# An attention and MLP kernel whose instruction order is laid out by a list scheduler of its own

## The chip, the core and the metric

The kernel runs on one core of a Trainium2 chip. A core has five engines with a queue each: TensorE (PE, matrix multiplication; its weight loads are shown as PEld), VectorE (DVE), ScalarE (ACT), GpSimd (POOL), and SyncE (SP), which here only issues DMA transfers. Each engine works through its own queue in the order in which the program was written out, and waits at an instruction until that instruction's inputs are there. The metric is the device time of one execution in microseconds.

## The reference

Four batches, eight heads, 768 positions, head size 64. Queries and keys are assigned to one of 16 centroids per head; a query attends only to keys with its own centroid. The attention output, as 3072 tokens of 512 numbers, goes through an MLP with 2048 hidden units.

```python
q_assign = np.argmax(np.einsum('bhsd,hcd->bhsc', q_n, c_n), axis=-1)
k_assign = np.argmax(np.einsum('bhsd,hcd->bhsc', k_n, c_n), axis=-1)
mask = q_assign[:, :, :, None] == k_assign[:, :, None, :]
scores = np.where(mask, scale * np.matmul(q, k.transpose(0, 1, 3, 2)), -1000000000.0)
attn = softmax(scores)                       # written out in the reference
x = matmul(attn, v) as (B * S, H * D)
g = s * np.maximum(x @ w_in, 0.0) ** 2 + b
out = g @ w_out
```

Inputs are float32. Most products are computed as three float16 products of a high and a low part.

## The kernel before

The work is cut into 192 attention units, each one head and 128 query positions of one batch (`units`), and 192 MLP steps, eight for each of 24 token tiles of 128 (`steps`; step m computes two of the 16 hidden tiles).

A unit `i` goes through these lines. `scores` (L492): four matmuls of 384 columns into one of two PSUM tiles `sc`; the one-hot encoding of the centroids rides along as extra rows (`KB`, `QB`), so that it masks. `maxima` (L501): the row maximum, VectorE. `exps` (L508, L511): a bias on VectorE, then the exponential on ScalarE into `p`. `high` (L519): the high half `ph` on ScalarE. `low` (L533, L535): the low half on GpSimd, and a transposing DMA from `ph` into `PT`. `values` (L552 to L564): for two units together, 36 matmuls into `px`, and the division on VectorE. Every fourth unit `finish_x` (L584 to L592) makes the MLP's input `x` through another transposing DMA, and every eighth, one matmul `am_x` (in `allmax`, L107) spreads a maximum over the partitions. The first 16 units ("raw") skip the halves: they are turned on TensorE in float32 (L530, L547), and the first two token tiles of the MLP are computed in float32 as well (L629, L673).

An MLP step runs `mlp_in` (L633, 24 matmuls of 128 columns into `h`), every second step `mlp_relu` (L646 to L649, ScalarE) and `mlp_g` (L661, GpSimd), and `mlp_out` (L676, six matmuls of 512 columns into `acc`); the end of a token tile is scaled on VectorE (L688) and stored (L690). Step m runs beside unit m + 14, its output three steps later (`LAG`, `BEHIND`).

Beside these run generators, advanced a little at each unit: `prep_q`, `prep_k` and `prep_v` prepare the next q, k and v (loads, maxima, halves, transposing DMAs into `QA`, `QB`, `KA`, `KB`; small matmuls `pq` L426 and `pk` L381 into a PSUM tile; `onehot` L309 to L315), `weights` decodes the 32 weight tiles (`fetch`, `rebase` L211 to L213 on ScalarE, `narrow` L217 and L218 on VectorE, `bound` L231 to L239), `wsplit` (L286 to L290) splits them into float16 halves.

Buffers come from rings named by a tag. Twelve "big" buffers hold `p`, `ph`, `PT`, `r` and the raw q. In PSUM there are two `sc`, one `acc`, one `h`, and two "m" tiles, which `px`, `pq`, `pk`, `am` and the weights' `pw` share.

The order of the queues comes from the framework's scheduler, which simulates the program with its own durations and takes what is ready by priority, the position in the program. The kernel steers it by hand in four ways: `first_of_all` moves the units 0 to 19 300 places forward; `behind(...)` holds instructions of the start behind others on the same engine (the one-hot, the turned tiles, the scale, the split); `gated` does so for the weights; and `load` holds each load behind the last transposing DMA.

Of the kernel before, what the change touches and what calls it, by code (L numbers as in the profile page):

```python
# [24 lines left out]

@with_exitstack
def tile_cluster_attention_mlp(ctx, tc, q, k, v, cent, w_in, w_out, s_in, b_in, out):
# [14 lines left out]
    V = nc.vector  # L42
    G = nc.gpsimd
    A = nc.scalar
# [33 lines left out]
    last_transpose = [None]  # L78
    last_split = [None, None]
    last_scale = [None]  # L80
    last_hot = [None]
    hot = [None]
    turned = [None]
    last_turn = [None]
    last_score = [None]
    last_max = [None]
    last_exp = [None]
# [15 lines left out]
    def allmax(dst, src, name):  # L103
        n = src.shape[1]
        pm = ps_m.tile([P, 512], F32, tag="m", name=f"am_{name}")
        for j in range(n):
            nc.tensor.matmul(pm[:, j * P : (j + 1) * P], src[:, j : j + 1].broadcast_to([P, P]), identb, start=True, stop=True)  # L107
        V.tensor_reduce(dst, pm[:, : n * P].rearrange("p (n q) -> p n q", q=P), axis=AX.X, op=ALU.max)
# [24 lines left out]
    def scalar_in(src, name):  # L133
        every = const([P, 1], F32, name)
        nc.sync.dma_start(every, src.partition_broadcast(P))
        return every

    def behind(*last):
        stack = ExitStack()
        for ins in last:  # L140
            if ins is not None:
                stack.enter_context(tc.issue_after(ins.ins))
        return stack

# [3 lines left out]
    nc.sync.dma_start(cn, cent.rearrange("h c d -> (h c) d"))  # L148
# [23 lines left out]
    for e in range(3):  # L172
        nc.tensor.matmul(pc[:, e * P : (e + 1) * P], cnat[:, e].rearrange("p e d -> p (e d)"), ident16, start=True, stop=True)
# [16 lines left out]
    def split(hi, lo, src, f):  # L190
        last_split[1] = A.activation(hi, src, AF.Copy, scale=f)
        yield
        V.scalar_tensor_tensor(lo, src, f, hi, op0=ALU.mult, op1=ALU.subtract)
# [29 lines left out]
    def bound(d):  # L223
        w, p, ft = d["w"], d["p"], d["ft"]
        top = w.bitcast(BF16).rearrange("p a (f z) -> p a f z", z=2)[:, :, :, 1]
        if p % 2:
# [4 lines left out]
            nc.tensor.matmul(sums[g], ones, top, start=ft in (0, EARLY), stop=done)  # L231
            if done:
                V.tensor_reduce(glob[:, 8 + g : 9 + g], sums[g], axis=AX.X, op=ALU.max)
        else:
            pw = ps_m.tile([P, 512], F32, tag="m", name=f"pw_{ft}")
            for t in range(KT):
                nc.tensor.matmul(pw[:, :P], ones, top[:, t, :], start=(t == 0), stop=(t == KT - 1))  # L237
# [7 lines left out]
    def gated(i):  # L245
        return behind(hot[0], turned[0]) if i < 20 else nullcontext()

    def weights():
        live = {}
        for i in range(2 * NF + 3):  # L250
            if 0 <= i - 3:
                with behind(last_score[0] if i < 20 else None):
                    bound(live[i - 3])
                narrowed[0] += 1
            if 0 <= i - 2 < 2 * NF:
                with gated(i):
                    narrow(live[i - 2])
            if i < 2 * NF:
                live[i] = fetch(i)
            if 0 <= i - 1 < 2 * NF:  # L260
                with gated(i):
                    rebase(live[i - 1])
# [32 lines left out]
    def column_sums():  # L295
        pb = ps_m.tile([P, 512], F32, tag="m", name="pb")
        for ft in range(NF):
            for e in range(2):
                nc.tensor.matmul(pb, ones16, WSP[ft][1][:, e, :], start=(ft + e == 0), stop=(ft + e == NF))
# [4 lines left out]
    def onehot(pa, nb, name, dst, mul, add):  # L304
# [10 lines left out]
        last_hot[0] = V.tensor_scalar(dst, o.unsqueeze(2).broadcast_to([P, nb, 4, C]), mul, add, op0=ALU.mult, op1=ALU.add)  # L315
# [3 lines left out]
    def turn(dst, src, early):  # L319
        if not early:  # L320
            return nc.sync.dma_start_transpose(dst, src)
        n = dst.shape[1]
        for a in range(0, n, 8):
# [4 lines left out]
            for j in range(a, z):  # L328
                nc.tensor.transpose(pt[:, (j - a) * P : (j - a + 1) * P], src[:, j * P : (j + 1) * P], ident16)
            last_turn[0] = A.activation(dst[:, a:z].rearrange("p n q -> p (n q)"), pt[:, : (z - a) * P], AF.Copy)  # L330
# [12 lines left out]
    def prep_k(b, hp):  # L343
# [18 lines left out]
        last_scale[0] = inverse2(V, sm[3], sm[2], 22)  # L362
# [3 lines left out]
        last_split[0] = G.tensor_copy(kb[:, :, :, 0, :], ka[:, :, :, 0, :])  # L366
# [9 lines left out]
        for h in range(2):  # L376
            hc = slice((2 * hp + h) * C, (2 * hp + h + 1) * C)
            for t in range(T):
                i = h * T + t
                o = pa[:, i * C : (i + 1) * C]  # L380
                nc.tensor.matmul(o, KA[:, i, :], cT[:, 0, hc], start=True, stop=False)  # L381
                nc.tensor.matmul(o, KA[:, i, :], cT[:, 1, hc], start=False, stop=True)
# [4 lines left out]
    def prep_q(b, c, hq):  # L387
# [21 lines left out]
        last_split[1] = A.activation(qb[:, :, 0, :], rows, AF.Copy)  # L409
        yield  # L410
        eng = G if b + c else V
        last_split[0] = eng.tensor_tensor(qa[:, :, 0, :], rows, qb[:, :, 0, :], op=ALU.subtract)
# [8 lines left out]
        for h in range(nh):  # L421
            hc = slice((nh * hq + h) * C, (nh * hq + h + 1) * C)
            for t in range(QT):
                i = h * QT + t
                o = pa[:, i * C : (i + 1) * C]
                nc.tensor.matmul(o, QA[:, i, :], cT[:, 0, hc], start=True, stop=False)  # L426
                nc.tensor.matmul(o, QA[:, i, :], cT[:, 2, hc], start=False, stop=True)
# [9 lines left out]
    def prep_v(b):  # L437
# [10 lines left out]
        for hp in range(NP):  # L448
            with behind(last_max[0] if b == 0 else None):
                absmax(vm[:, hp : hp + 1], vns[hp].rearrange("p h t d -> p (h t d)"))  # L450
# [32 lines left out]
    def scores(i):  # L483
# [5 lines left out]
        for X, Y, st in ((QA, KA, True), (QB, KB, False)):  # L489
            y = Y.rearrange("p n q -> p (n q)")  # L490
            for e in range(2):
                last_score[0] = nc.tensor.matmul(  # L492
# [4 lines left out]
    def maxima(i):  # L497
# [3 lines left out]
        last_max[0] = V.tensor_reduce(SM[i // 4][:, 0, j : j + 1], U[i]["sc"], axis=AX.XY, op=ALU.max, negate=True)  # L501

    def exps(i):
# [7 lines left out]
        last_exp[0] = A.activation(p.rearrange("p (a b) -> p a b", a=2), u["sc"], AF.Exp, bias=bi, scale=u["scale"], **total)  # L511
# [9 lines left out]
    def low(i):  # L521
        u = U[i]
        if i < RAW:
# [3 lines left out]
            for e, (pool, bank) in enumerate(((ps_h, "h"), (ps_m, "m"))):  # L527
                back = pool.tile([P, 512], F32, tag=bank, name=f"turned_{i}_{e}")
                for kt in range(n):
                    nc.tensor.transpose(back[:, kt * P : (kt + 1) * P], u["p"][:, (e * n + kt) * P : (e * n + kt + 1) * P], ident)  # L530
# [4 lines left out]
        last_transpose[0] = nc.sync.dma_start_transpose(u["PT"], u["ph"].rearrange("p e s -> p (e s)"))  # L535

    def values(i):
# [3 lines left out]
        for e in range(2):  # L541
# [3 lines left out]
            if i < RAW:  # L545
                for kt in range(T):
                    nc.tensor.matmul(o, PT[:, kt, :], VN[hp][:, h, kt, :], start=(kt == 0), stop=(kt == T - 1))  # L547
# [3 lines left out]
            for kt in range(T):  # L551
                nc.tensor.matmul(o1, PT[:, kt, :], vh[:, h, kt, : D + 1], start=(kt == 0), stop=False)  # L552
                nc.tensor.matmul(o, PT[:, kt, :], vl[:, h, kt, :], start=False, stop=False)  # L553
                nc.tensor.matmul(o1, PT[:, T + kt, :], vh[:, h, kt, : D + 1], start=False, stop=(kt == T - 1))  # L554
# [12 lines left out]
    def finish_x(g):  # L567
# [3 lines left out]
        if 4 * g < XRAW:  # L571
            xt = ps_m.tile([P, 512], F32, tag="m", name=f"xt_{g}")
            for j in range(2):
                nc.tensor.transpose(xt[:, j * P : (j + 1) * P], xs[:, j].rearrange("p h d -> p (h d)"), ident)
# [14 lines left out]
        nc.sync.dma_start_transpose(x.rearrange("p j e q -> p (j e) q"), xn.rearrange("p j e h d -> p (j e h d)"))  # L589
# [28 lines left out]
    def mlp_in(n, m):  # L618
# [3 lines left out]
        for j in range(2):  # L622
            ft = 2 * m + j
            o = ph[:, (2 * (m % 2) + j) * P :][:, :P]
            if plain(n):
                while narrowed[0] < 2 * ft + 2:
                    next(wgen, None)
                for kt in range(KT):
                    nc.tensor.matmul(o, wi[ft][:, kt, :], XS[(n, kt // 2)][:, kt % 2, :], start=(kt == 0), stop=(kt == KT - 1))  # L629
                continue  # L630
            terms = [(kt, wl, xl) for kt in range(KT) for wl, xl in ((0, 0), (0, 1), (1, 0))]
            for i, (kt, wl, xl) in enumerate(terms):
                nc.tensor.matmul(o, WSP[ft][0][:, wl, kt, :], XS[(n, kt // 2)][:, kt % 2, xl, :],  # L633
# [30 lines left out]
    def mlp_out(n, m):  # L664
# [4 lines left out]
        for j in range(2):  # L669
            ft = 2 * m + j  # L670
            rows = slice((2 * (m % 2) + j) * P, (2 * (m % 2) + j + 1) * P)
            if plain(n):
                nc.tensor.matmul(acc, g[:, rows], wo[ft].rearrange("p a f -> p (a f)"), start=(ft == 0), stop=(ft == NF - 1))  # L673
                continue
            for gl, wl in ((0, 0), (0, 1), (1, 0)):
                nc.tensor.matmul(acc, g[:, gl, rows], WSP[ft][1][:, wl, :],  # L676
# [3 lines left out]
        if m == STEPS - 1:  # L680
# [9 lines left out]
            nc.sync.dma_start(out[b * S : (b + 1) * S].rearrange("(p t) e -> p t e", t=T)[:, t, :], o)  # L690
# [31 lines left out]
    def first_of_all(k):  # L722
        return tc.high_priority(offset=300) if k < URGENT else nullcontext()

# [9 lines left out]
    def prepare(k):  # L734
        with behind(hot[0]):
            if k == 1:
                run(first_q[1])
                run(first_k[2])
            if k == 3:
# [120 lines left out]
```

## Time and profile before

| | |
|---|---|
| median of 3 runs | 994.08 us (992.73 to 995.89) |
| profiled execution | 997.6 us |
| its span, first to last instruction | 995.7 us |
| TensorE busy | 868.6 us, 87% of the span |
| VectorE busy | 643.5 us, 65% |
| ScalarE busy | 630.0 us, 63% |
| GpSimd busy | 519.2 us, 52% |
| mean granted TensorE clock | 0.963 |
| DMA queue of the data, share of 16 engines | 72.5% |

The span is what the trace covers. "Busy" leaves out waiting and the issuing of transfers. In the rows below, an instruction is named by the engine, the tile it writes and the line; `out<-in` names the tiles; x is a count; the number after the bar is the total busy time in us, then the mean of one in ns, then the idle time of the engine just before such instructions and what ended it. The granted clock is the share of full speed at which TensorE was let run.

### The profile page before, as it was taken

To read this page: it belongs to the slowest core of one execution; us is meant where nothing else is said; L and a number is where in the kernel's file an instruction comes from. 1 tells how busy PE (TensorE), PEld (TensorE's weight loads), DVE (VectorE), ACT (ScalarE), POOL (GpSimd) and SP (SyncE) were. 2 spreads that over 40 slices of the span, in tenths; PEclk is the share of its full clock that TensorE was granted. 3 is DMA by queue.
4 is the path that set the end of the run, shared out by engine and by line. 5 is a ranking of instruction groups with operands and counts; after the bars stand their busy time and mean duration, and the time that the engine had idled before them with its cause. 6 is when DMAs were issued, how large, how long until landed. Compare 5 with 4: busy or idle time off the path is not lost.

```text
span 995.7 us, 26540 instructions
## 1 busy us (share of the span) xinstructions
PE 868.6 (87%) x10883; PEld 646.2 (65%) x10885; DVE 643.5 (65%) x1704; ACT 630.0 (63%) x921; POOL 519.2 (52%) x443
## 2 busy tenths in 40 slices
PE   2547799988898989989888989989869989999997
PEld 2336677756566767766666767766656767767775
DVE  7868974797868564657776655576676565564420
ACT  4768865658656667656557666666557667667632
POOL 2225433335555656655465666665556566566631
PEclk9968799999999999999999999999999999999999
DMA  5824436648789878788989679789979778777730
GB/s 175 306 70 159 123 59 103 153 80 165 142 160 159 151 124 149 141 168 160 182 139 176 128 130 144 154 170 164 176 146 168 122 131 138 144 129 121 125 56 22
DMA packets 400682, 139.66 MB, mean 140 GB/s; under 512 B 386224, under 2 KB 386224, under 8 KB 400560
## 3 DMA queue, kind: packets, MB, share of 16 engines
q1 hardware_dynamic: 400560, 137.97, 72.5%
q8 instruction: 85, 1.39, 0.6%
q14 instruction: 37, 0.30, 0.1%
HBM read 35.69 MB, written 6.29 MB: 42 GB/s over the span
## 4 chain that ended last, share of the span: by engine, by line
PE 38%; DVE 18%; issue 14%; DMA 12%; POOL 11%; ACT 6%; SPq 1%; POOLq 0%; ACTq 0%; DVEq 0%
PE h L633 12%; PE acc L676 11%; POOL ph L533 5%; PE sc L492 5%; DVE ssm L501 3%; DMA qn<-in_q_dram 3%; DMA PT<-ph 2%; POOL g L661 2%; PE px L552 2%; ACT ph L519 2%; PE px L554 2%; DMA QA<-qa 2%; PE px L553 2%; DMA QB<-qb 1%; ACT p L511 1%
## 5 line engine op out<-in xcount | busy, mean ns | idle before, releaser
L533 POOL TENSOR_TENSOR ph<-p,ph 128x768 f16<-128x768 f32 x176 | 292.2, 1661 | 275.1 <-ACT ph L519 263.7
L511 ACT ACTIVATE p<-sc,ssm,qsm 128x768 f32<-128x768 f32 x192 | 189.3, 986 | 167.7 <-DVE ssm L508 94.4
L633 PEld LDWEIGHTS <-ws 128*128 128x128 f16 x4224 | 258.3, 99 | 42.3 <-issue 4.7
L676 PE MATMUL acc<-ws,g 128*128 128x512 f16 x1056 | 267.9, 382 | 13.3 <-POOL g L661 12.4
L633 PE MATMUL h<-x,ws 128*128 128x128 f16 x4224 | 277.5, 221 | 1.1 <-DVE ws L289 0.7
L501 DVE TENSOR_REDUCE ssm<-sc 128x1 f32<-128x768 f32 x192 | 182.5, 951 | 89.3 <-PE sc L492 89.1
L519 ACT ACTIVATE ph<-p 128x768 f16<-128x768 f32 x176 | 147.1, 836 | 27.4 <-DMA PT<-ph 15.6
L676 PEld LDWEIGHTS <-g 128*128 128x128 f16 x1056 | 96.9, 98 | 101.0 <-POOL g L661 15.9
L661 POOL TENSOR_TENSOR g<-r,g 128x512 f16<-128x512 f32 x88 | 104.1, 1183 | 29.7 <-ACT r L649 16.5
L552 PE MATMUL px<-vh,PT 128*128 128x65 f16 x1056 | 113.3, 197 | 3.1 <-DMA PT<-ph 1.1
L492 PE MATMUL sc<-KA,QA 128*128 128x384 f16 x384 | 97.1, 335 | 19.1 <-ACT p L511 18.1
L553 PE MATMUL px<-vl,PT 128*128 128x64 f16 x1056 | 113.1, 194 | 0.0
L554 PE MATMUL px<-vh,PT 128*128 128x65 f16 x1056 | 112.6, 195 | 0.0
L552 PEld LDWEIGHTS <-PT 128*128 128x128 f16 x1056 | 99.5, 99 | 8.3 <-issue 3.1
L492 PE MATMUL sc<-KB,QB 128*128 128x384 f16 x384 | 102.4, 335 | 1.7 <-DMA QB<-qb 1.1
L553 PEld LDWEIGHTS <-PT 128*128 128x128 f16 x1056 | 99.4, 100 | 4.2 <-issue 1.0
L554 PEld LDWEIGHTS <-PT 128*128 128x128 f16 x1056 | 99.4, 98 | 0.9
L646 ACT ACTIVATE r<-h,cf 128x512 f32<-128x512 f32 x88 | 60.1, 683 | 47.2 <-PE h L633 45.6
L239 POOL TENSOR_TENSOR w<-w,wsg 128x512 f32<-128x512 f32 x32 | 41.1, 1289 | 72.6 <-PE pw L237 33.2
L560 DVE TENSOR_SCALAR ssm<-px 128x2 f32<-128x2 f32 x88 | 13.5, 154 | 88.3 <-PE px L554 88.3
L492 PEld LDWEIGHTS <-QA 128*128 128x128 f16 x384 | 32.1, 100 | 42.0 <-issue 26.0
L587 POOL TENSOR_TENSOR xn<-xs,xn 128x256 f16<-128x256 f32 x44 | 31.5, 717 | 47.2 <-ACT xn L584 47.0
(167 smaller groups left out, 1271.5 us busy)
## 6 DMA issues: line engine op xcount, KB each, us to landing
wst<-in_moe_w_in_dram SPq DMA_DIRECT2D x16, 512.0 KB, 4.7
wst<-in_moe_w_out_dram SPq DMA_DIRECT2D x16, 512.0 KB, 5.0
kn<-in_k_dram SPq DMA_DIRECT2D x16, 384.0 KB, 4.1
qn<-in_q_dram SPq DMA_DIRECT2D x24, 256.0 KB, 4.3
vn<-in_v_dram SPq DMA_DIRECT2D x16, 384.0 KB, 4.0
out_dram<-o SPq DMA_DIRECT2D x24, 256.0 KB, 2.3
PT<-ph SPq DMA_TRANSPOSE x176, 3.9
x<-xn SPq DMA_TRANSPOSE x44, 2.9
```

The source lines that it names most:

```text
L492: last_score[0] = nc.tensor.matmul(sc[:, e, :HALF], X[:, col, :], y[:, h * S + e * HALF : h * S + (e + 1) * HALF], start=st, stop=not st)
L501: last_max[0] = V.tensor_reduce(SM[i // 4][:, 0, j : j + 1], U[i]["sc"], axis=AX.XY, op=ALU.max, negate=True)
L511: last_exp[0] = A.activation(p.rearrange("p (a b) -> p a b", a=2), u["sc"], AF.Exp, bias=bi, scale=u["scale"], **total)
L519: A.activation(u["ph"][:, 0, :], u["p"], AF.Copy)
L533: G.tensor_tensor(u["ph"][:, 1, :], u["p"], u["ph"][:, 0, :], op=ALU.subtract)
L552: nc.tensor.matmul(o1, PT[:, kt, :], vh[:, h, kt, : D + 1], start=(kt == 0), stop=False)
L553: nc.tensor.matmul(o, PT[:, kt, :], vl[:, h, kt, :], start=False, stop=False)
L554: nc.tensor.matmul(o1, PT[:, T + kt, :], vh[:, h, kt, : D + 1], start=False, stop=(kt == T - 1))
L633: nc.tensor.matmul(o, WSP[ft][0][:, wl, kt, :], XS[(n, kt // 2)][:, kt % 2, xl, :], start=(i == 0), stop=(i == len(terms) - 1))
L646: A.activation(r, ph, AF.Relu, scale=MS[n][0])
L661: G.tensor_tensor(g[:, 1, :], r, g[:, 0, :], op=ALU.subtract)
L676: nc.tensor.matmul(acc, g[:, gl, rows], WSP[ft][1][:, wl, :], start=(ft == 0 and gl + wl == 0), stop=(ft == NF - 1 and gl == 1))
```

## The change

The kernel body no longer issues instructions. Its engines are replaced by recorders (`V`, `G`, `A`, `M`, `S_`), and every call becomes a `Step` with the tiles that it reads and writes; from overlapping bytes the plan derives which earlier steps it must wait for. Matmuls in a row that write the same tile with the same weight tile become one step. At the end `plan.emit()` walks the steps in time with durations of its own: `takes` for the compute engines, `transfer` for DMAs. On each engine, among the steps whose inputs are done, it takes the one that can start first; those that could start within 30 ns of the engine coming free count as equal, and the earlier in the program goes first. A step can start only when its tiles have a buffer, and the buffers of a tag are given in the order in which the program first mentions them. It also models that VectorE and GpSimd exclude each other for some operations, and that no more than eight transfers are under way. The instructions are then issued in the order of their planned start, and the framework is told to keep it.

All hand-made steering is removed: `behind`, `gated`, `first_of_all`, the holding back of loads, and the variables that remembered instructions for it.

```diff
+class Plan:
+    LIGHT = 2.4
+    SIGNAL = 40.0
...
+    def record(self, queue, method, args, kwargs):
...
+        key = (id(writes[0].tensor), id(reads[0].tensor)) if queue.name == "PE" else None
+        step = self.last_pe
+        if key is None or step is None or step.key != key:
+            step = Step()
...
+    def takes(self, step):
+        method, args, kwargs = step.calls[0]
+        aps = [a for a in args if isinstance(a, bass.AP)]
+        if step.queue.name == "PE":
+            total = 0.0
+            for _, args, _ in step.calls:
+                n = self.width(args[0])
+                if args[1].dtype == F32:
+                    total += max(n * 4 / self.LIGHT, 112.0)
+                else:
+                    total += 56.0 if n == P else max(n / self.LIGHT + 2.5, 26.0)
+            return total, False
...
+        if name == "DVE":
+            if method in ("tensor_reduce", "reciprocal"):
+                return 145 + n / 0.96, method == "reciprocal" and not banks
+            if method == "tensor_tensor":
+                return 148 + n / 0.96, not banks
+            if method == "scalar_tensor_tensor":
+                return (200.0 if n == 1 else 165 + n * 1.1), not banks
+            fold = 1 if banks else 4 if small else 2
+            return 150 + n / 0.96 / fold, not banks
+        if name == "ACT":
+            more = 110 if "accum_out" in kwargs else 0
+            if banks:
+                return (170 + n * 0.84 if small else 140 + n * 1.1 if n > 700 else 130 + n * 0.97) + more, False
+            return (100 + n * 1.1 if args[2] == AF.Copy and "scale" in kwargs else 100 + n * 1.0) + more, False
+        if method == "tensor_tensor":
+            return 165 + n * 1.93, True
+        if method == "tensor_copy":
+            return 60 + n * 1.35, True
+        return 100.0, True
+
+    def transfer(self, step):
...
+        if method == "dma_start":
+            n = P * self.width(ap) * (2 if ap.dtype in (F16, BF16) else 4)
+            return 420.0, 1300.0, n / 410.0, 1050.0
+        n = self.width(ap) // P
+        return (1300.0 if n < 12 else 1480.0), 1300.0, n * 165.0, 500.0
+
+    def order(self):
...
+        while left:
+            best = None
+            for q, line in pending.items():
+                now = clock[q]
+                choice = None
+                for k in line:
+                    at, need = max(ready[k], now), {}
+                    for t in steps[k].tiles:
+                        if t.name in held:
+                            continue
+                        tag = self.tag(t)
+                        if turn[t.name] != given[tag] + need.get(tag, 0) or len(spare[tag]) <= need.get(tag, 0):
+                            at = None
+                            break
+                        at = max(at, spare[tag][need.get(tag, 0)])
+                        need[tag] = need.get(tag, 0) + 1
+                    if at is None:
+                        continue
+                    if q == "SP" and len(landed) >= 8:
+                        at = max(at, landed[-8])
+                    mine = (max(at, now + 30), self.weight[k], at, k)
+                    if choice is None or mine < choice:
+                        choice = mine
+                if choice and (best is None or choice[2] < best[2]):
+                    best = choice + (q,)
...
+            for j in after[k]:
+                open_[j] -= 1
+                same = steps[j].queue.name == q == "PE"
+                ready[j] = max(ready[j], end - 60 if same else end + self.SIGNAL)
...
+        return sorted(range(len(steps)), key=lambda k: (started[k], k))
...
+    def emit(self):
+        self.weight = [s.rank for s in self.steps]
+        for k in self.order():
+            s = self.steps[k]
+            for method, args, kwargs in s.calls:
+                self.tc.keep_in_program_order(getattr(s.queue.engine, method)(*args, **kwargs))
...
-    V = nc.vector
-    G = nc.gpsimd
-    A = nc.scalar
+    plan = Plan(tc)
+    V = plan.queue("DVE", nc.vector)
+    G = plan.queue("POOL", nc.gpsimd)
+    A = plan.queue("ACT", nc.scalar)
+    M = plan.queue("PE", nc.tensor)
+    S_ = plan.queue("SP", nc.sync)
...
-    def load(dst, src, free=False):
-        if last_transpose[0] is None or free:
-            nc.sync.dma_start(dst, src)
-        else:
-            with tc.issue_after(last_transpose[0].ins):
-                nc.sync.dma_start(dst, src)
+    def load(dst, src):
+        S_.dma_start(dst, src)
...
-    def gated(i):
-        return behind(hot[0], turned[0]) if i < 20 else nullcontext()
...
-                with behind(last_score[0] if i < 20 else None):
-                    bound(live[i - 3])
+                bound(live[i - 3])
...
-                with gated(i):
-                    narrow(live[i - 2])
+                narrow(live[i - 2])
...
-    def first_of_all(k):
-        return tc.high_priority(offset=300) if k < URGENT else nullcontext()
...
         if i < NU:
-            with first_of_all(i):
-                scores(i)
+            scores(i)
...
+    plan.emit()
```

More of the change, by code (lines that the diff above doesn't have):

```diff
@@ L1 @@
 import math
[L2 removed]
+import heapq
 import concourse.bass as bass
@@ L134, in scalar_in @@
         every = const([P, 1], F32, name)
-        nc.sync.dma_start(every, src.partition_broadcast(P))
+        S_.dma_start(every, src.partition_broadcast(P))
         return every
[L138 to L143, printed above, removed]
     ct = sb.tile([P, 2, D], F32, tag="r", name="ct", bufs=2)
     cn = ct[:, 0, :]
-    nc.sync.dma_start(cn, cent.rearrange("h c d -> (h c) d"))
+    S_.dma_start(cn, cent.rearrange("h c d -> (h c) d"))
     csq = ct[:, 1, :]
@@ L230, in bound @@
             done = ft in (EARLY - 1, NF - 1)
-            nc.tensor.matmul(sums[g], ones, top, start=ft in (0, EARLY), stop=done)
+            M.matmul(sums[g], ones, top, start=ft in (0, EARLY), stop=done)
             if done:
@@ L236, in bound @@
             for t in range(KT):
-                nc.tensor.matmul(pw[:, :P], ones, top[:, t, :], start=(t == 0), stop=(t == KT - 1))
+                M.matmul(pw[:, :P], ones, top[:, t, :], start=(t == 0), stop=(t == KT - 1))
             V.tensor_reduce(w1[:, ft : ft + 1], pw[:, :P], axis=AX.X, op=ALU.max)
@@ L448, in prep_v @@
         for hp in range(NP):
-            with behind(last_max[0] if b == 0 else None):
-                absmax(vm[:, hp : hp + 1], vns[hp].rearrange("p h t d -> p (h t d)"))
+            absmax(vm[:, hp : hp + 1], vns[hp].rearrange("p h t d -> p (h t d)"))
             if hp < NP - 1:
@@ L546, in values @@
                 for kt in range(T):
-                    nc.tensor.matmul(o, PT[:, kt, :], VN[hp][:, h, kt, :], start=(kt == 0), stop=(kt == T - 1))
+                    M.matmul(o, PT[:, kt, :], VN[hp][:, h, kt, :], start=(kt == 0), stop=(kt == T - 1))
                 continue
@@ L734, in prepare @@
     def prepare(k):
[L735 to L739, printed above, removed]
-                run(first_k[3])
-            if k == 2:
-                some(first_v, 2)
-            if k == 6:
-                active.append(first_v)
+        if k == 1:
+            run(first_q[1])
+            run(first_k[2])
+        if k == 3:
+            run(first_k[3])
+        if k == 2:
+            some(first_v, 2)
+        if k == 6:
+            active.append(first_v)
     first_v = prep_v(0)
@@ L754, in tile_cluster_attention_mlp @@
     some(first_k[0], 2)
-    with behind(last_scale[0]):
-        some(first_k[1], 1)
-        some(first_q[0], 1)
+    some(first_k[1], 1)
+    some(first_q[0], 1)
     some(first_k[0], 1)
```

266 lines of the change are left out of this document (202 added, 64 removed).

## The prediction

> **What bounds the kernel now.** I read the page's busy shares and slices first, then a table of four stages, then the waits of TensorE inside the long middle stage.
>
> ```profile
> span 995.7 us, 26540 instructions
> PE 868.6 (87%) x10883; PEld 646.2 (65%) x10885; DVE 643.5 (65%) x1704; ACT 630.0 (63%) x921; POOL 519.2 (52%) x443
> PE   2547799988898989989888989989869989999997
> DVE  7868974797868564657776655576676565564420
> PEclk9968799999999999999999999999999999999999
> ```
>
> TensorE is the only engine near its limit, but not from the beginning: its first five slices (125 us) run at 2 to 7 tenths, while VectorE runs at 6 to 9 there.
>
> The stages, from the table of stretches (us; busy time and count of each engine, then granted clock, DMA share and GB/s):
>
> ```profile
> 0.00:125.00 125.00, 71.79 (x601) 56.74 (x604) 104.67 (x260) 87.67 (x152) 43.92 (x67) 0.85 0.49 167
> 125.00:200.00 75.00, 72.41 (x619) 56.80 (x618) 47.83 (x105) 45.96 (x71) 27.35 (x20) 1.00 0.53 102
> 200.00:950.00 750.00, 683.87 (x9194) 503.99 (x9193) 486.17 (x1323) 482.39 (x677) 438.05 (x349) 0.98 0.83 146
> 950.00:995.70 45.70, 40.53 (x478) 28.69 (x475) 4.83 (x18) 13.94 (x22) 9.90 (x10) 0.98 0.16 33
> ...
> 425.00:450.00 25.00, 21.31 (x289) 15.79 (x290) 15.77 (x52) 14.88 (x22) 13.36 (x11) 0.93 0.84 164
> 575.00:600.00 25.00, 21.05 (x294) 15.77 (x292) 13.80 (x43) 15.91 (x22) 14.20 (x12) 0.93 0.71 127
> 825.00:850.00 25.00, 25.00 (x325) 18.24 (x324) 11.32 (x32) 18.08 (x25) 14.92 (x12) 1.00 0.87 145
> 900.00:925.00 25.00, 25.00 (x357) 18.84 (x354) 12.16 (x36) 18.52 (x27) 15.18 (x12) 1.00 0.75 123
> ```
>
> Three readings. In the start VectorE is busy 104.67 of 125 us, so it sets the pace and has 125 - 104.67 = 20.3 us of holes. From 200 to 950 TensorE is idle 750 - 683.87 = 66.1 us and its mean clock is 0.98, which costs about 2% of 750 = 15 us more: 81 us in all that an ideal order could recover, since nothing else is above 65% busy there. And the stretches 825:850 and 900:925 show that this pipeline, with these buffers, can hold TensorE at 25.00 of 25. The tail and the stage 125:200 have little to give.
>
> Who TensorE waits for between 200 and 950 (us in total, times, longest):
>
> ```profile
> PE am_x L107 <- DVE amb_x L592: 15.5, 7, 3.4
> PE sc L492 <- ACT p L511: 13.3, 11, 2.4
> PE acc L676 <- POOL g L661: 11.5, 15, 1.5
> PE pq L426 <- DMA QA<-qa: 11.2, 7, 3.3
> PE am_k L107 <- DVE amb_k L111: 2.9, 3, 1.3
> PE acc L673 <- DVE g L658: 2.9, 1, 2.9
> PE am_x L107 <- DVE oe_q L310: 1.6, 2, 0.9
> ```
>
> These are 58.9 of the 66.1 us. All have one form: the instruction at the head of TensorE's queue waits for a VectorE chain, a GpSimd subtraction or a transfer that was expected sooner. They are errors of the present queue order, not missing work.
>
> **The change, part by part.** It removes no arithmetic and no transfer. Matmul counts, shapes, buffers and DMAs stay, so the sum is a sum over waits. Four things change: the durations by which the order is made; the hand-made gates and priorities of the start; the order in which buffers are handed out; the grain at which matmuls are placed.
>
> *New durations.* The order is now made from formulas in the diff. I compare them with the rows of the operations behind the waits.
>
> ```profile
> L661 POOL TENSOR_TENSOR g<-r,g 128x512 f16<-128x512 f32 x88 | 104.1, 1183 | 29.7 <-ACT r L649 16.5 <-issue 9.9 <-PE acc L676 3.3
> L511 ACT ACTIVATE p<-sc,ssm,qsm 128x768 f32<-128x768 f32 x192 | 189.3, 986 | 167.7 <-DVE ssm L508 94.4 <-PE px L554 13.3 <-DMA PT<-ph 10.3
> L111 DVE TENSOR_REDUCE xm<-xs 128x1 f32<-128x256 f32 x44 | 18.0, 409 | 0.1
> QA<-qa SPq DMA_TRANSPOSE x22, 3.5
> QB<-qb SPq DMA_TRANSPOSE x22, 4.5
> PT<-ph SPq DMA_TRANSPOSE x176, 3.9
> ```
>
> GpSimd: 165 + 512 x 1.93 = 1153 ns against 1183. ScalarE exponential: 140 + 768 x 1.1 = 985 against 986. VectorE maximum: 145 + 256 / 0.96 = 412 against 409. Transposes: QA 1300 + 8 x 165 + 500 = 3.12 us against 3.5, QB the same 3.12 against 4.5, PT 3.78 against 3.9. So compute operations are priced within 3%, transfers up to 1.4 us short. I take, wait by wait: `acc` on GpSimd goes wholly (11.5); `sc` on ScalarE two thirds (9 of 13.3), because the exponential is right but queues behind work of other lines; the `am` waits half (10 of 15.5 + 2.9 + 1.6 = 20.0), because their VectorE chain is priced well but their PSUM buffer is handed out in a strict order (below); `pq` on the transfer half (5.6 of 11.2), because the price is short; the `L673` wait and the 7.2 us not listed, nothing. Sum 11.5 + 9 + 10 + 5.6 = 36.1 us. The clock follows the stalls: 36 of 66 of the 15 us is 8. Middle stage: -44, at most -81.
>
> The Trainium skill ("TensorE: Matmul & The Clock Gate", section "Part 1: The HAM clock gate") says the clock halves after an idle window of about 3.4 us, and asks for no idle gaps above that. By that rule the middle stage, whose longest listed wait is 3.4 us, has almost no clock loss and the 8 us fall away. The rows disagree: 425:450 and 575:600 are at 0.93. I go by the rows.
>
> *Wrong price of f32 matmuls.* The formula takes four passes. From the chain of waits:
>
> ```profile
> 165.31 1.72 PE acc L673 x4
> 167.03 1.78 PE h L629 x16
> ```
>
> with, in the groups:
>
> ```profile
> L629 PE MATMUL h<-x,w 128*128 128x128 f32 x256 | 32.1, 276 | 0.0
> L673 PE MATMUL acc<-w,g 128*128 128x512 f32 x64 | 31.5, 624 | 2.9 <-DVE g L658 2.9
> ```
>
> One 128-column f32 matmul takes 1.78 / 16 = 111 ns, the formula 128 x 4 / 2.4 = 213; one of 512 takes 430, the formula 853. The plan holds TensorE busy 256 x 0.102 + 64 x 0.423 = 53 us too long in the raw stage, and puts other engines' work ahead of the MLP's that it believes to be free. At the stage's VectorE density (47.83 of 75) that is 53 x 0.64 = 34 us of VectorE work against 75 - 47.83 = 27 us of holes: cost between 0 and 7, taken at +3.
>
> *Gates and priorities taken out of the start.* The narrowing of 32 weight tiles loses its wait for the first one-hot and the first turned tiles, and units 0 to 19 lose their 300-place head start. VectorE sets the pace there, and the new rule never leaves it idle while something can start. Best case: the holes of 20.3 us go. Worst case: narrowing comes between the links of the first chain.
>
> ```profile
> L218 DVE SCALAR_TENSOR_TENSOR w<-wst,w 128x512 uint32<-128x512 uint32 x32 | 25.7, 811 | 0.2
> L217 DVE TENSOR_SCALAR w<-w 128x512 int32<-128x512 int32 x32 | 15.6, 494 | 0.5 <-ACT w L211 0.5
> ```
>
> One tile costs 811 + 494 = 1305 ns; eight of them ahead of the first scores are +10 us. Since that work has to be done in this stage anyway, most is given back. Between -20 and +10 I take -10: half the holes. Loads also stop waiting behind the last issued transpose; behind a load on the SyncE queue stand the PT transposes and, after them, TensorE's `px`. I cost that at nothing: SyncE's plan holds only what can start, and the cover is TensorE's other work; without the cover one PT landing, 3.9 us, per misplaced load.
>
> *Grain.* Matmuls that share a written tile and a weight tile are now placed as one block (twelve of `h`, 18 of `px`), which starts when its last input is there. A `px` block reads one transposed tile and an `h` block the x of one token tile, so its first and last matmul become ready nearly together; I cost it at nothing, and what covers it is again TensorE's other work.
>
> *Buffers in program order.* Each ring hands out its buffers strictly in the order of first mention. The two PSUM buffers named "m" serve `px`, `pq`, `pk` and `am_x`: a `px` whose PT has landed must let a `pq` go first whose QA is still travelling. Whether the present scheduler does the same no row shows. I cost it inside the halves above; its full price is the third rival.
>
> **Sum.** Against the profiled execution's own 997.6 us (span 995.7 and 1.9 around it): -44 middle, -10 start, +3 raw stage = 946.6. The median of the runs, 994.1, lies 3.5 below that execution: 943.
>
> **Rivals.**
> First, *nearly everything is recovered*: -81 and -20 give 997.6 - 101 - 3.5 = 893. For it: 25.00 of 25 at 900:925. Against it: that stretch has no q, k, v preparation left, and the transfers are priced short.
>
> Second, *the DMA engines take it back*. Share 0.83 over 750 us; 81 us shorter makes 0.93, 44 us shorter 0.88, and a transpose then queues behind others. For it: 3.5 and 4.5 us for QA and QB of one size, so queueing exists. Against it: 0.87 at 825:850 with TensorE full. If half of middle and start goes: 997.6 - 22 - 7 - 3.5 = 965.
>
> Third, on the other side: *the ring of two "m" buffers, in strict program order, becomes the stall*. There are 22 + 12 turns of `pq` and `pk` that wait for a transpose and 22 of `am_x`. At today's mean wait (11.2 / 7 = 1.6 us; 15.5 / 7 = 2.2 us) all of them would cost 34 x 1.6 + 22 x 2.2 = 102 us against 26.7 now: +75. The forecast's other terms keep 11.5 + 9 + about 5 of clock + 7 of start = 32. Decisive from 32 / 1.8 = 18 stalled turns beyond today's 14; with all 56 the time is 997.6 + 75 - 32 - 3.5 = 1037, with two thirds of the extra 1012. For it: these are the waits already there. Against it: TensorE has `h`, `acc` and `sc` to do meanwhile.
>
> Fourth, *the order hardly changes*: the rank is the program position, as now, so the list may come out nearly the same: 994.
>
> **How the numbers follow.** A measurement of this kernel can tell about 0.3% (3 us) from no change. Forecast 0.47, its own range 920 to 962; nearly everything 0.12; DMA 0.15; ring 0.20; same 0.06. Faster: 0.47 + 0.12 + 0.15 = 0.74; same 0.06; slower 0.20. The range leaves out the best tenth below 902 and the worst tenth above 1012.
>
> **What would show it.** Right: TensorE's idle time in the middle falls from 66 to about 30 us, the `acc` on `g` wait to under 3, granted clock above 0.98, VectorE above 0.88 in the first 125 us. Ring: waits of `px`, `pq` or `am` grow past 60 us together. DMA: share over 0.9 with PT landing above 4.5 us. Raw stage wrong: TensorE under 70 of 75 us after the start. The forecast fails altogether if the start lengthens by more than 44 us, or the waits only change their names.

## The result and the profile after

The changed kernel takes 943.0 us (median of 4 runs, 940.64 to 945.36) against 994.99 us before; the ratio is 0.9461, with a 95% interval of 0.9395 to 0.9527. The forecast was 943. The total was right; two of its terms were not, and they cancelled, as the stages show. The profiled execution took 945.36 us, its span 943.7.

The page after, with three rows of its list of transfers (all lines now carry L289, the one place that issues):

```profile
span 943.7 us, 26567 instructions
PE 860.8 (91%) x10885; PEld 644.1 (68%) x10885; DVE 642.9 (68%) x1704; ACT 628.8 (67%) x921; POOL 521.5 (55%) x443
PE   1659779999889999999989999999989999999997
...
QA<-qa SPq DMA_TRANSPOSE x22, 3.6
QB<-qb SPq DMA_TRANSPOSE x22, 3.4
PT<-ph SPq DMA_TRANSPOSE x176, 4.1
```

Busy times are those of before within 1%: the same work in a shorter span.

The stages after, in the columns of the table of before; the tail again has 45.7 us:

```profile
0.00:125.00 125.00, 73.27 (x587) 55.57 (x588) 99.86 (x251) 86.27 (x151) 43.65 (x67) 0.80 0.50 169
125.00:200.00 75.00, 73.54 (x555) 58.97 (x555) 51.90 (x112) 43.41 (x68) 27.11 (x20) 0.92 0.50 102
200.00:898.00 698.00, 673.71 (x9275) 501.40 (x9274) 486.26 (x1325) 485.17 (x682) 441.31 (x349) 0.99 0.90 157
898.00:943.70 45.70, 40.28 (x474) 28.17 (x470) 4.83 (x18) 13.93 (x22) 9.47 (x10) 0.99 0.17 32
```

TensorE's idle time in the middle fell from 66.1 to 698 - 673.71 = 24.3 us, its clock rose from 0.98 to 0.99, and 81 more matmuls fell into this stage. In the start VectorE, which I had expected to be busier, is busy 4.8 us less, and TensorE's granted clock is lower: 0.80 and 0.92 in the first two stages against 0.85 and 1.00 before.

Where the time came from is plainest by progress. Counting TensorE's score matmuls in the trace, four to a unit, the scores of a unit begin at (us):

```
unit      before   after   difference
  0         18.8    28.3      +9.6
 16        127.0   139.4     +12.5
 24        179.1   185.2      +6.0
 32        223.2   222.8      -0.3
 64        380.3   367.7     -12.5
128        665.1   631.0     -34.2
160        818.2   766.7     -51.5
191        941.5   890.4     -51.1
```

So the start lost 6 us up to unit 24. From there to the last unit 762.4 us became 705.2, which is -57; all of it is gained by unit 160, and nothing behind it.

TensorE's waits in the middle, after:

```profile
PE sc L289 <- ACT p L289: 9.2, 7, 2.5
PE acc L289 <- POOL g L289: 4.8, 4, 3.4
PE px L289 <- DMA PT<-ph: 2.6, 4, 1.1
PE px L289 <- DVE xs L289: 2.4, 2, 1.4
PE pq L289 <- DMA QA<-qa: 1.8, 4, 0.7
```

`am` (20.0 us before) is no longer in the list, `pq` fell from 11.2 to 1.8, `acc` from 11.5 to 4.8.

One thing stands only in VectorE's waits, which the prediction leaves out. Before, then after, over the whole span:

```profile
DVE qsm L111 <- DMA qn<-in_q_dram: 40.4, 14, 6.0
DVE amb_k L111 <- DMA kn<-in_k_dram: 22.8, 7, 5.1
DVE vm L111 <- DMA vn<-in_v_dram: 21.0, 7, 4.4
```

```profile
DVE qsm L289 <- DMA qn<-in_q_dram: 6.6, 4, 2.9
DVE amb_k L289 <- DMA kn<-in_k_dram: 1.3, 2, 0.8
```

VectorE stood 84 us at maxima of data that were still being loaded, with the row maxima of later units behind them in its queue; after, 8 us.

### The profile page after: what moved, and what is told of

The parts are those of the page before. It is cut to its first block, busy times and chain, and to the rows that moved or that the text cites. A ratio compares the mean times of both kernels' runs of the same rounds, so it can differ in the third digit from the quotient of the medians.

```text
span 943.7 us, 26567 instructions
## 1 busy us (share of the span) xinstructions
PE 860.8 (91%) x10885; PEld 644.1 (68%) x10885; DVE 642.9 (68%) x1704; ACT 628.8 (67%) x921; POOL 521.5 (55%) x443
## 5 line engine op out<-in xcount | busy, mean ns | idle before, releaser
L289 POOL TENSOR_TENSOR ph<-p,ph 128x768 f16<-128x768 f32 x176 | 295.0, 1677 | 231.8 <-ACT ph L289 209.9
L289 PEld LDWEIGHTS <-ws 128*128 128x128 f16 x4224 | 252.1, 99 | 32.8 <-issue 5.1
L289 PE MATMUL h<-x,ws 128*128 128x128 f16 x4224 | 266.0, 220 | 2.5 <-DMA x<-xn 1.4
L289 PE MATMUL acc<-ws,g 128*128 128x512 f16 x1056 | 257.0, 380 | 7.2 <-POOL g L289 6.1
L289 DVE TENSOR_REDUCE ssm<-sc 128x1 f32<-128x768 f32 x192 | 183.0, 953 | 101.2 <-PE sc L289 100.6
L289 ACT ACTIVATE p<-sc,ssm,qsm 128x768 f32<-128x768 f32 x192 | 188.7, 983 | 91.3 <-DVE ssm L289 51.9
L289 PEld LDWEIGHTS <-g 128*128 128x128 f16 x1056 | 97.7, 98 | 105.4 <-POOL g L289 9.4
L289 ACT ACTIVATE ph<-p 128x768 f16<-128x768 f32 x176 | 146.9, 835 | 21.5 <-DMA PT<-ph 13.8
L289 POOL TENSOR_TENSOR g<-r,g 128x512 f16<-128x512 f32 x88 | 102.9, 1170 | 45.4 <-ACT r L289 33.3
L289 PE MATMUL px<-vh,PT 128*128 128x65 f16 x2112 | 113.5, 194 | 5.0 <-DMA PT<-ph 2.6
L289 PEld LDWEIGHTS <-PT 128*128 128x128 f16 x3168 | 107.2, 98 | 11.7 <-issue 3.6
L289 PE MATMUL sc<-KA,QA 128*128 128x384 f16 x384 | 96.6, 335 | 15.6 <-ACT p L289 15.4
L289 PE MATMUL px<-vl,PT 128*128 128x64 f16 x1056 | 107.3, 192 | 0.0
L289 PE MATMUL sc<-KB,QB 128*128 128x384 f16 x384 | 96.7, 335 | 0.5 <-ACT QB L289 0.5
L289 ACT ACTIVATE r<-h,cf 128x512 f32<-128x512 f32 x88 | 59.9, 680 | 43.7 <-PE h L289 31.5
L289 POOL TENSOR_TENSOR w<-w,wsg 128x512 f32<-128x512 f32 x32 | 40.0, 1261 | 70.5 <-PE pw L289 43.6
L289 PEld LDWEIGHTS <-QA 128*128 128x128 f16 x768 | 44.5, 99 | 40.0 <-issue 21.7
L289 DVE TENSOR_SCALAR ssm<-px 128x2 f32<-128x2 f32 x88 | 13.8, 157 | 80.2 <-PE px L289 79.5
L289 ACT ACTIVATE g<-r 128x512 f16<-128x512 f32 x88 | 55.1, 626 | 1.9
L289 ACT ACTIVATE r<-r 128x512 f32<-128x512 f32 x88 | 54.7, 622 | 1.3
L289 PEld LDWEIGHTS <-QB 128*128 128x128 f16 x384 | 37.2, 100 | 24.1 <-issue 1.9
L289 POOL TENSOR_TENSOR xn<-xs,xn 128x256 f16<-128x256 f32 x44 | 30.5, 693 | 32.5 <-ACT xn L289 26.8
```

The source lines that it names most:

```text
L289: self.tc.keep_in_program_order(getattr(s.queue.engine, method)(*args, **kwargs))
```

## The experiments

The theory: the order follows from the durations in the plan, and those that match the chip make the gain in the middle. The rivals: freed loads; a better priority list, whatever the durations; any list scheduling at all. Ratios are to the kernel before on the same chip, with 95% intervals. Gains and losses in us are plain differences to the changed kernel's 943.0. The experiments ran on three chips, on which the kernel before took 993.3 to 997.1 us, and the changed kernel's own interval is 13 us wide (0.9395 to 0.9527), so a few us between two kernels settle nothing.

**The framework's durations on the plan's order (e1).**

```diff
-                self.tc.keep_in_program_order(getattr(s.queue.engine, method)(*args, **kwargs))
+                getattr(s.queue.engine, method)(*args, **kwargs)
```

> The steps are recorded, planned and issued in the planned order as in the changed kernel, but the framework is not told to keep that order: its own scheduler lays out the queues again, with its own durations, taking the planned position as priority. Theory (the durations make the gain): the framework's durations bring the old waits of TensorE back, `acc` on the GpSimd subtraction over 8 us and `am` and `pq` over 12 us between 200 us and the tail, and the time is 970 to 1000 us. Rival (a better priority list is what counts): 940 to 955 us.

968.5 us, ratio 0.9731 (0.9703 to 0.9760). The time is just below the theory's range and 13.5 us above the rival's. The wait for transposed q is back; `acc`, which the theory had over 8 us, is at 3.5 and is not. VectorE waits 46 us for q, k and v loads. TensorE's waits in the middle:

```profile
PE pq L289 <- DMA QA<-qa: 13.2, 7, 6.6
PE px L289 <- DMA PT<-ph: 6.2, 5, 2.2
PE am_x L289 <- DVE amb_x L289: 5.7, 3, 2.2
```

About half of the gain (27 of 52 us) comes without keeping the order; the other half needs it.

**Two prices made wrong together, then each alone (e2, e5, e6, e7).** In the same plan:

```diff
-            return 165 + n * 1.93, True                                # e2, e5
+            return 85 + n * 0.97, True
...
-        return (1300.0 if n < 12 else 1480.0), 1300.0, n * 165.0, 500.0   # e2, e6
+        return (1300.0 if n < 12 else 1480.0), 650.0, n * 83.0, 250.0
...
-            return 420.0, 1300.0, n / 410.0, 1050.0                      # e7
+            return 420.0, 300.0, n / 820.0, 250.0
```

> The changed kernel with two prices made wrong: GpSimd's tensor_tensor at half (85 + 0.97 n ns) and the transposing DMAs at half (landing of a 12-column PT 1.9 instead of 3.8 us). Everything else as changed. Theory (the durations make the gain): TensorE's waits for POOL g and for transposed tiles between 200 us and the tail grow from 9 us to over 30 us, and 25 to 60 us of the gain are lost: 968 to 1003 us. Rival (any list scheduling with buffers in program order would do): 940 to 950 us.

1017.8 us, ratio 1.0227 (1.0191 to 1.0264): 75 us lost, more than expected, and slower than the kernel before. "Any list scheduling" is out. TensorE's waits in its middle:

```profile
PE acc L289 <- POOL g L289: 28.8, 19, 2.4
PE am_x L289 <- DVE amb_x L289: 19.2, 10, 3.6
PE h L289 <- ACT r L289: 17.8, 14, 4.4
PE am_k L289 <- DVE xs L289: 13.2, 3, 5.4
```

The expected growth for transposed tiles did not show, and the 28.8 us for `g` alone fall just short of the 30 expected of both. Alone, each price shows its own wait.

> The changed kernel with one price wrong: GpSimd's tensor_tensor at half (85 + 0.97 n ns); transposes and loads priced as changed. With both GpSimd and transposes short the time was 75 us longer and TensorE waited 26.7 us for `g`. Theory (the GpSimd price is the term that carries most, as the 11.5 us in the sum): 975 to 1005 us, TensorE's wait for POOL g over 15 us. Rival (the transposes' price carries most): 943 to 955 us.

987.6 us, 0.9935 (0.9915 to 0.9955), so 45 us of the gain lost; it lies within what the theory expected.

```profile
PE acc L289 <- POOL g L289: 23.7, 17, 3.0
PE sc L289 <- ACT p L289: 11.6, 9, 4.1
```

The wait named in the theory, `acc`, grew by 19 us, of the 45 lost. Something else came with it: VectorE's waits for q, k and v loads are 68 us here and 75 us in e2, although loads are priced as in the changed kernel.

> The changed kernel with one price wrong: transposing DMAs at half (650 + 83 n + 250 ns), all else as changed. Theory (GpSimd carries most): 948 to 965 us, with TensorE's waits for QA and PT over 12 us between 200 us and the tail against 4.4 now. Rival (the transposes' price carries most): 985 to 1010 us.

981.3 us, 0.9877 (0.9849 to 0.9904): 38 us lost, between both expectations. Transposes weigh nearly as much as GpSimd, which I had put well ahead.

```profile
PE pq L289 <- DMA QA<-qa: 29.7, 16, 3.9
```

> The changed kernel with one price wrong: plain loads and stores planned to land 1.8 us and half their size earlier (300 + n/820 + 250 instead of 1300 + n/410 + 1050 ns). VectorE waited 84 us for q, k and v loads in the kernel before and 8 us in the changed one. New theory, not in the prediction (the plan's load price keeps VectorE from queueing a maximum ahead of its data, and that is a good part of the gain): VectorE's waits for loads return to 50 us or more and the time is 955 to 980 us. Rival (those waits lie beside VectorE's slack, since it is only 65 to 70% busy): 941 to 950 us.

972.2 us, 0.977 (0.9732 to 0.9807): 29 us lost, as the new theory said, with VectorE's waits at 42 us, not quite the 50 expected. Its first scores also came 8.4 us later than the changed kernel's and unit 24 5.6 us later, so part of the 29 is the start. And since the same waits return in e2 and e5, they do not point to the price of loads alone.

```profile
DVE qsm L289 <- DMA qn<-in_q_dram: 40.1, 16, 6.9
DVE amb_k L289 <- DMA kn<-in_k_dram: 1.6, 3, 0.8
DVE vm L289 <- DMA vn<-in_v_dram: 0.7, 1, 0.7
```

Each of three prices, halved or cut, costs 29 to 45 us; the losses of e5 and e6 nearly add up (45 + 38 = 83 against 75 in e2). No run changes a price that should not matter, or makes one of these three too long, so how far such an order moves by mere chance is not known; that `acc` and `pq` each grow with their own price speaks against chance for these two.

**Loads free in the kernel before, and held in the plan (e3, e8).**

```diff
-        if last_transpose[0] is None or free:      # e3, in the kernel before
+        if True:
...
-        S_.dma_start(dst, src)                     # e8, in the changed kernel
+        step = S_.dma_start(dst, src)
+        if last_transpose[0] is not None:
+            step.waits.add(last_transpose[0].rank)
```

> The kernel before, with one part of the steering taken out: loads are no longer held behind the last transposing DMA. Theory (the durations make the gain): 988 to 998 us, no clear change. Rival (the gain comes from loads that go out earlier): 945 to 970 us, with VectorE's waits for the q, k and v loads (84 us before) more than halved.

984.6 us, 0.9895 (0.9874 to 0.9916). Free loads alone are worth 11 us, below the theory's range and far above the rival's. VectorE's waits for q rose from 40.4 to 50.3 us, those for k and v fell from 43.8 to 18.1, so 84 us became 68 in all, and the rival's halving did not come. Which of these makes the 11 us is not shown.

> The changed kernel with the old holding of loads put back into the plan as an edge: each load is planned behind the transposing DMA of a unit's halves recorded last before it. Freeing the loads in the kernel before gave 10.6 us. Theory (the gain of free loads is part of the gain here as well): 948 to 956 us. Rival (a plan that knows when a load lands does not need it early): 941 to 946 us.

965.9 us, 0.9714 (0.9693 to 0.9735), 23 us lost, more than either side expected. Unit 64 began 4.1 us earlier than in the changed kernel, unit 191 20.4 us later, and TensorE waits for the transposes (15.1 us, against 2.6 in the changed kernel):

```profile
PE px L290 <- DMA PT<-ph: 15.1, 10, 2.7
PE sc L290 <- ACT p L290: 9.6, 11, 2.0
```

The landing time of PT is 4.1 us there too, so it is not the transfer that got slower. In the trace, 23 of the 176 PT transposes go out more than 2 us after GpSimd has finished their `ph`, against 15 in the changed kernel; in front of the late ones (over 1 us) on SyncE stands most often a transpose of `qb` (15 of 45, against 8 of 48), and a load less often than in the changed kernel (5 against 12). That the held q loads bring these transposes of `qb` into the way fits, but was not tested.

**The start (e4, e11).** The old gates become edges of the plan (an edge is an order of two steps that the plan has to keep), the head start an earlier rank, that is, an earlier place in the program; e11 also holds the loads.

```diff
+        for h in self.holds:
+            if h.queue is queue and h is not step:
+                step.waits.add(h.rank)
...
+            step.ready = step.rank - self.ahead     # 100 for the units 0 to 19
...
-        self.weight = [s.rank for s in self.steps]
+        self.weight = [s.ready for s in self.steps]
```

> The changed kernel, to whose plan the hand steering of the start is given back as extra edges and as a head start of 100 steps for the units 0 to 19 (the loads stay free). Theory (the start lost 9.6 us to its first scores because weight tiles came between the links of the first chain): first scores before 22 us instead of 28.3, and 4 to 10 us less in all: 933 to 939 us. Rival (VectorE's amount of work sets the start, whatever its order): 940 to 946 us, with the first scores earlier and the unit 24 at the same time as in the changed kernel.

938.2 us, 0.9415 (0.9379 to 0.9451). First scores at 19.0, unit 24 at 177.6 instead of 185.2 us, as the theory said; the interval overlaps the changed kernel's, so the 5 us in the time are not settled. In the profile the units from 24 on stay 7 to 13 us ahead to the end, but e4's profiled execution is the shortest of its four (932.7 us), the changed kernel's the longest of its four.

> The plan and the kept order of the changed kernel, with all of the old hand steering put back into it as edges and a head start: the gates of the start and the loads behind the transposes. Theory (the two halves of the steering act as measured apart: gates -5 us, held loads +23 us): 955 to 966 us. Rival (a plan with right prices makes the steering nearly irrelevant, and the 23 us of the held loads came from the start): 938 to 950 us.

969.6 us, 0.9721 (0.9688 to 0.9755), 4 us above the theory's range and clear of the rival's. Unit 24 is 6.8 us earlier than in the changed kernel, unit 191 19.9 later. Taking the whole steering out of the plan is worth 27 us; held loads alone make 23 of them (e8), and the gates give nothing in the time when the loads are held.

**The price of f32 matmuls (e9).**

```diff
-                    total += max(n * 4 / self.LIGHT, 112.0)
+                    total += max(n * 2 / self.LIGHT + 2.5, 112.0)
```

> The changed kernel with the f32 matmuls priced at two passes (128 columns 112 ns, 512 columns 429 ns) instead of four. Theory (the prediction's step: the wrong price costs 3 us, 0 to 7): 936 to 943 us, and TensorE's granted clock in 100 to 150 us above the 0.70 and 0.75 of the changed kernel. Rival (the order of the raw stage is bound by VectorE and hardly depends on it): 941 to 946 us.

957.4 us, 0.9611 (0.9581 to 0.9642): the right price is 14 us slower, outside both expectations. TensorE's granted clock rose only in one of the two stretches that the theory named (0.70 in both kernels at 100:125, 0.95 against 0.75 at 125:150). Unit 24 comes 2.1 us earlier, unit 64 7.8 later. The changed kernel, then e9, where they part:

```profile
150.00:175.00 25.00, 25.00 (x171) 19.26 (x170) 19.14 (x30) 15.18 (x23) 9.27 (x6) 1.00 0.59 113
225.00:250.00 25.00, 22.63 (x273) 16.81 (x272) 24.66 (x50) 20.95 (x31) 14.18 (x11) 0.93 0.62 118
```

```profile
150.00:175.00 25.00, 25.00 (x181) 18.68 (x181) 11.28 (x23) 13.12 (x20) 7.49 (x5) 1.00 0.50 106
225.00:250.00 25.00, 18.80 (x226) 13.78 (x227) 24.95 (x47) 18.93 (x28) 11.66 (x8) 0.86 0.65 122
```

With the wrong price VectorE does 7.9 us more work between 150 and 175, while TensorE is full anyway. At 225:250 VectorE is full in both kernels, and without that lead TensorE loses 3.8 us more there. The lead at 150:175 is mostly the preparation of v (instructions on `vn`: 6.13 against 0.80 us of VectorE) and the weight split (on `ws`: 7.01 against 2.96). That it makes the 10 us between the units 24 and 64 fits, but was not tested apart.

**The strict ring of "m" buffers (e10, e13).**

```diff
-                        if turn[t.name] != given[tag] + need.get(tag, 0) or len(spare[tag]) <= need.get(tag, 0):
+                        if (tag not in free and turn[t.name] != given[tag] + need.get(tag, 0)) or len(spare[tag]) <= need.get(tag, 0):
```

with `free` the tag of `px`.

> The changed kernel, but the two PSUM buffers named m are given to whichever step can start first, not in the order of first mention. Theory (the strict order costs little, because with the right prices the plan gets to each turn in time; the third rival did not come about): 939 to 946 us, no clear change. Rival (the strict ring still holds TensorE back, half of its am and pq waits): 925 to 937 us.

926.7 us, 0.9299 (0.9269 to 0.9328): 16 us faster than the changed kernel and clear of it. The theory fell. The time lies in the rival's range, but not where the rival put it: most of the gain lies in the start. In the profile (e10's shortest execution of six) unit 0 is 5.1 us earlier, unit 16 17.3, unit 24 17.5, and the last one 21.8. The first maximum of keys on VectorE and TensorE's first instructions in the changed kernel, with VectorE's at 13.99 and 14.34, then TensorE's in e10, then those of the kernel before:

```profile
4.85 0.96 DVE L289 TENSOR_REDUCE amb_k<-kn 128x1 bf16<-128x768 f32 x1 [0.81 <-DMA kn<-in_k_dram]
...
11.28 0.69 PE L289 MATMUL pc<-ident,cnat 128*128 128x128 f16 x3 [11.28 <-DVE cnat L289]
11.77 0.31 PE L289 MATMUL am_k<-identb,amb_k 128*128 128x128 bf16 x1
...
13.99 0.43 DVE L289 TENSOR_SCALAR w<-w 128x512 int32<-128x512 int32 x1 [2.37 <-ACT w L289]
14.34 0.28 DVE L289 TENSOR_REDUCE ksm<-am_k 128x1 f32<-128x128 f32 x1
...
19.12 2.31 PE L289 MATMUL turn<-ident,ka 128*128 128x128 f16 x20 [4.19 <-DVE ka L289]
...
28.35 1.49 PE L289 MATMUL sc<-KA,QA 128*128 128x384 f16 x4
```

```profile
5.91 0.29 PE L290 MATMUL am_k<-identb,amb_k 128*128 128x128 bf16 x1 [5.91 <-DVE cs L290]
...
10.35 1.46 PE L290 MATMUL turn<-ident,ka 128*128 128x128 f16 x12 [3.20 <-DVE ka L290]
11.61 0.53 PE L290 MATMUL pc<-ident,cnat 128*128 128x128 f16 x3
...
23.28 1.44 PE L290 MATMUL sc<-KA,QA 128*128 128x384 f16 x4
```

```profile
8.01 0.29 PE L173 MATMUL pc<-ident,cnat 128*128 128x128 f16 x1 [8.01 <-DVE cnat L165]
8.09 0.31 PE L107 MATMUL am_k<-identb,amb_k 128*128 128x128 bf16 x1
...
12.02 1.46 PE L329 MATMUL turn<-ident,ka 128*128 128x128 f16 x12 [1.33 <-DVE ka L193]
```

The program mentions the centroids' tile `pc` first, so it has the first turn in the ring, and its input is the end of a long VectorE chain. The spread of the first key maximum, `am_k`, has its data by 5.8 us, but gets its buffer after `pc`, at 11.77. Free, it runs at 5.91, and the keys are turned at 10.35 instead of 19.12.

The kernel before gave `pc` the first turn as well (8.01, then `am_k` at 8.09), so the ring alone does not explain why the changed kernel turns its keys 7.1 us later than before (19.12 against 12.02). Of these, 3.7 us stand in front of `am_k`: in VectorE's queue five maxima of k and q lie among the steps that lead to `pc`, where one lay before. The other 3.4 us come behind it: `am_k` is done by 12.1, but VectorE stands 2.37 us at a weight tile `w` whose input is late, with `ksm`, the step that needs `am_k`, behind it in the queue. With the gates (e4) the strict ring is kept, and the first scores come at 19.0 all the same.

The first scores account for 5.1 of the 17.5 us that e10 is ahead at unit 24. The rest comes between the units 0 and 24. VectorE's longest wait in the first 125 us of the changed kernel,

```profile
DVE xs L289 <- PE px L289: 8.8, 4, 3.2
```

is for `px`, which shares the ring, and it is gone in e10; VectorE is busy 108.5 us there instead of 99.86, and TensorE's granted clock is 0.88 instead of 0.80. How the 12 us divide among the turns of `px` and the clock was not tested.

> The changed kernel with two edits: the m buffers free in order, and the gates of the start put back as plan edges (without the head start of 100 steps, with which the plan finds no step that can begin). Each alone took time from the start: 17 us (m free) and 5 to 12 us (gates with head start), both before unit 24. Theory (they remove different delays: the ring holds TensorE's turns, the gates keep weight tiles out of the first chain): 918 to 924 us. Rival (both buy the same holes of the start): 924 to 932 us.

927.4 us, 0.9312 (0.9280 to 0.9343): nothing beyond e10, as the rival said. The first scores come 3.5 us earlier than in e10 but unit 24 5.8 later, so the gates still shorten the first chain and lose more than that behind it; where was not traced. A run with the free ring, the gates with their head start and the right f32 price together (e12; expected 930 to 938 us) gave no time: with the head start and the free ring the plan comes to a point where no step can begin. The best kernel is e10, 16 us ahead of the changed one.

## Why the prediction was right, and where it was not

*What bounds the kernel.* Right. The middle lost 66 us to errors of order, and the same queues with better prices gave back 42 of idle time; with wrong prices (e2, e5, e6) the waits return under the same names. Of the signs set for a right forecast, two came (idle time near 30 us, clock above 0.98) and two did not (`acc` under 3 us, VectorE above 0.88 in the first 125 us).

*New durations, -44.* Right in mechanism, somewhat small: the middle stage shrank by 52 us, and from unit 24 on it is -57. It is the whole middle that is measured, so freed loads, the grain and the ring lie in it too: e8 puts the free loads at 23 us, e10 the ring at 4, and no run changes the grain. Wait by wait it was mixed. `am` went wholly, where I took half; `pq` by five sixths, where I took half; `sc` kept 9.2 us, where I left 4.3, and `acc` 4.8, where I left none. The idle time I expected, "about 30", was 24.3. I also missed a term: the 76 us in which VectorE no longer stands at loads. I used the waits of the engine that bounds, and the loads stood in the queue of the engine that feeds it. e7 loses 29 us with such waits back at 42 us, but they also return in e2 and e5, so their own price is not shown.

*The clock, 8 us.* Right: 2% of 750 us, 15, became 1% of 698, 7. The stretch of 675 to 700 us, whose longest TensorE wait is 2.5 us (for `sc`), again has 0.93; in it the 3 us from 687 on, just behind that wait, which ends at 685.94, have 0.50. So the loss begins below the 3.4 us that the Trainium skill ("TensorE: Matmul & The Clock Gate", section "Part 1: The HAM clock gate") names.

```profile
675.00:700.00 25.00, 20.82 (x326) 16.57 (x327) 15.67 (x52) 16.38 (x23) 16.13 (x15) 0.93 0.92 154
```

*Gates and priorities, -10.* Wrong, and the sign with it. The step that failed is "the new rule never leaves it idle while something can start", from which I took half of VectorE's 20.3 us of holes. VectorE's holes grew from 20.3 to 25.1 us. The rule holds in the plan's own time only, and only for steps that have a buffer. On the chip VectorE stood 2.37 us at a late weight tile with a step of the first chain behind it, which is the worst case that the prediction itself named; and the strict ring kept steps from starting (with it free, in e10, the holes are 16.5 us). The start lost 6 us instead of gaining 7 net.

*Wrong f32 price, +3.* The sign was wrong: that price saves 14 us (e9). I treated work that the plan moves ahead as a cost; as far as the rows show, it was done while TensorE was full anyway, ahead of a stage in which VectorE is full.

*Loads, costed at nothing.* Wrong: 11 us in the old order, 23 in the plan. TensorE's waits for PT did grow, from 2.6 to 15.1 us, but a late transpose rarely has a load just in front of it (e8).

*Buffers in program order.* I priced the ring in the middle, where e10 gained only 4 us, and not in the start, where it cost 17. That no row shows what the scheduler before does with the ring is not so: `am_k`, whose input was there by 5.4 us, ran behind `pc` at 8.09. As the third rival put it, it did not come: `px`, `pq` and `am` together wait 7 us.

*The second rival.* The DMA share did rise to 0.90, but PT lands in 4.1 us against 3.9, short of the 4.5 that I had named. Its sum also took the whole of the start's net gain, 7 us, and not half of it; with half it comes to 969 us instead of 965.

So -57 and +6 make -51, where I had -44 and -7. Two errors of some 13 us cancelled, and the hit of 943 says less than it seems.

## What to carry to other kernels

A fixed queue order depends on its durations: here one wrong by half, for one kind of operation, cost 3 to 5% of the kernel, so they are to be checked against rows for every engine and for transfers, loads among them. A truer price is still no promise of a better order: the right price of f32 matmuls cost 1.5%. Read the waits of the engines that feed the bounding one too, since an instruction at the head of their queue holds up everything behind it. Where buffers are handed out in program order, see what the program mentions first: a tile with a late input takes the turn of all that follow; in the start of this kernel that was not covered.

## What the runs showed of the hardware that was not expected

TensorE's granted clock was 0.93 in a stretch of 25 us with one wait of 2.5 us and two of about 1 us, with 0.50 in the 3 us from 687 on, just behind the longest. And the middle ran with a DMA share of 0.90 instead of 0.83 while the median landing of PT only went from 3.9 to 4.1 us.
